# Four normalizations of the last row group spread over VectorE, GpSimd and ScalarE in a spectral-filter plus S²-MLP kernel

## The chip, the cores and the metric

The kernel runs on one core of a Trainium2 chip. The metric is the device time of one launch in microseconds (us). The core has a matrix engine (TensorE, PE in the profile, with weight loads on PEld), VectorE (DVE), ScalarE (ACT), GpSimd (POOL), and SyncE (SP), which in this kernel issues all DMAs. Every engine takes its instructions strictly in the order in which they stand in its queue; between engines, semaphores order the work.

## The reference, cut to what matters

```python
xn = layernorm(x)                                   # x: 2048 x 448, fp32
A  = irfft2(rfft2(xn) * (w_r + 1j * w_i))           # spectral filter
h  = gelu(layernorm(xn) @ w1)                       # 448 -> 448
x1 = xn + shift(h) @ w2                             # quarters of h moved by +1, -1, +2, -2 rows
B  = x1 + gelu(layernorm(x1) @ w3) @ w4             # 448 -> 1792 -> 448
return x + A + B
```

`layernorm` takes mean and variance over a row and has no learned weights.

## The kernel before

The 2048 rows are 16 blocks of 128 rows. Blocks are handled in four groups of four (`GRP`, line 22): group 0 is blocks 14, 15, 0, 1; group 1 is 2 to 5; group 2 is 6 to 9; group 3 is 10 to 13. Two blocks share one SBUF tile: blocks 10 and 11 are `xt5` (`xt_81` in the instruction rows), blocks 12 and 13 are `xt6` (`xt_82`). All matrix products run on fp16 pairs (a high part and a low part), three products for one.

Stages, in order: each group is normalized (`norm1`, line 319), turned so that features lie on partitions, and multiplied by `w1` (`w1_unit`, line 451; one unit is one block). A unit applies gelu and splits the result into high part (ACT, L461) and low part (DVE, L464), both written into `x2mem` at shifted places. When the neighbours of a block are there, a DMA transpose (L475) turns that block into a tile `h`, and `w2_tile` (line 480) multiplies it by `w2` on PE (L484, 11 matmuls of 128x448) and adds it to the block on DVE (L485, scaled by `cs`). After that come the second layer norm (`ln2`, line 488), the MLP by `w3` and `w4` (`front`, `back`), and the spectral part, whose matmuls are mixed with the MLP's. These last stages fill the time from about 70 us to the end.

`norm1(g, apply)` works out mean and variance of the four blocks on DVE (L306 to L328) and then applies them: `x * y + nm` per block, in place, on the engine that `apply` names for that block. `V` is VectorE, `P` is GpSimd (both L336, `tensor_scalar`), `A` is ScalarE (L333, an activation with scale and bias). It returns `refine` (L343 to L352), ten small GpSimd operations that sharpen the reciprocal root, which the caller runs later. `scales` (line 356) works out `cs` on GpSimd (L360 to L367).

Groups 0 to 2 are turned by PE (`T1`). Group 3 is turned by DMA: `turn(3)` (line 860) takes each block's high part on ACT (L866), its low part on DVE (L867, L868) and issues one DMA transpose per block into `xT` (L869). All DMA transposes of the kernel, L475, L520 and L869, and all plain DMAs stand in the one queue of SP.

The order in which instructions stand in each engine's queue is not written out: a scheduler places them at build time from its own estimate of the time, with priorities and with the `behind(...)` marks, which say after which instruction something may be issued. A different engine for one operation can thus move others.

PSUM banks are shared by tag, two of each: `sp` for the `w2` tiles (`pw2_0`, `pw2_1`, ...), so `pw2_2` needs the bank that L485 of `pw2_0` frees; `mm` and `acc` for the `w1` units of groups 2 and 3 (`pw1_20` is group 2, unit 0); `mm` and `tr` in turn for the first MLP tiles (`pw3_00`, `pw3_01`, ...).

Unit 0 of group 2 completes block 4 of `h` (`DONE`, line 27), which `pw2_4` reads; units 1, 2 and 3 complete blocks 5, 6 and 7. Unit 0 of group 3 completes block 8.

Of the kernel before, what the change touches and what calls it, by code (L numbers as in the profile page):

```python
# [125 lines left out]
def body(tc, nc, x, wf, w1, w2, w3, w4, c_g, c_n, c_small, out):  # L126
    V, A, P, T, SY = nc.vector, nc.scalar, nc.gpsimd, nc.tensor, nc.sync
# [40 lines left out]
    def xb(b):  # L168
        return xt[b // 2][:, b % 2]
# [130 lines left out]
    def stats(src, key, mv=None, pins=None):  # L300
        if mv is None:
            mv = pc.tile([128, 4, 2], F32, tag="mv", bufs=3, name=f"mv{key}")
        for i, s in enumerate(src):
            st = pc.tile([128, 6], F32, tag="st", bufs=4, name=f"st{key}_{i}")
            with behind(*pins[i]) if pins else contextlib.nullcontext():
                V.bn_stats(out=st, in_=s)  # L306
            V.bn_aggr(out=mv[:, i, :], in_=st)
        return mv
# [10 lines left out]
    def norm1(g, apply, pins=None):  # L319

        bs, c = GRP[g], slice(4 * g, 4 * g + 4)
        mv, a, y, nm = mva[:, c], va[:, :, c], vy[:, :, c], nma[:, c]
        stats([xb(b) for b in bs], f"a{g}", mv, pins)
        V.tensor_scalar(out=a[:, 1], in0=mv[:, :, 1], scalar1=1.0 + EPS, scalar2=EPS * EPS, op0=ALU.mult, op1=ALU.add)
        V.tensor_scalar(out=a[:, 0], in0=mv[:, :, 1], scalar1=EPS, scalar2=None, op0=ALU.add)
        V.tensor_single_scalar(vyi[:, :, c], va.bitcast(I32)[:, :, c], 1, op=ALU.logical_shift_right)
        V.tensor_scalar(out=vyi[:, :, c], in0=vyi[:, :, c], scalar1=-1, scalar2=0x5F3759DF, op0=ALU.mult, op1=ALU.add)
        i = V.scalar_tensor_tensor(out=nm, in0=mv[:, :, 0], scalar=-1.0, in1=y[:, 1], op0=ALU.mult, op1=ALU.mult)  # L328
        after["c", g] = (i.ins,)
        for k, b in enumerate(bs):  # L330
            y_, m_ = y[:, 1, k:k + 1], nm[:, k:k + 1]
            if apply[k] is A:
                i = A.activation(out=xb(b), in_=xb(b), func=AF.Identity, scale=y_, bias=m_)  # L333
                after["na", g] = (i.ins,)
            else:
                i = apply[k].tensor_scalar(out=xb(b), in0=xb(b), scalar1=y_, scalar2=m_, op0=ALU.mult, op1=ALU.add)  # L336
                after["n" if apply[k] is V else "np", g] = (i.ins,)

        q, z = (pc.tile([128, 2, 4], F32, tag=f"v{t}", bufs=2, name=f"v{t}{g}") for t in "qz")
        w, r = vw[:, :, c], vr[:, :, c]  # L340

        def refine():
            P.tensor_tensor(out=q, in0=y, in1=y, op=ALU.mult)  # L343
            P.tensor_tensor(out=q, in0=q, in1=a, op=ALU.mult)
            P.tensor_scalar(out=w, in0=q, scalar1=-10.0 / 3.0, scalar2=None, op0=ALU.add)
            P.tensor_tensor(out=w, in0=w, in1=q, op=ALU.mult)
            P.tensor_scalar(out=w, in0=w, scalar1=5.0, scalar2=None, op0=ALU.add)
            P.tensor_tensor(out=z, in0=w, in1=w, op=ALU.mult)
            P.tensor_tensor(out=z, in0=z, in1=q, op=ALU.mult)
            P.tensor_scalar(out=z, in0=z, scalar1=-0.5 * 0.375 ** 3, scalar2=1.5 * 0.375, op0=ALU.mult, op1=ALU.add)  # L350
            P.tensor_tensor(out=r, in0=z, in1=w, op=ALU.mult)
            i = P.tensor_scalar(out=gsc[:, c], in0=r[:, 1], scalar1=r1, scalar2=None, op0=ALU.mult)  # L352
            after["g", g] = (i.ins,)
        return refine
# [19 lines left out]
    @contextlib.contextmanager  # L374
    def behind(*key):
        key = key if len(key) > 1 else key[0]
        with contextlib.ExitStack() as st:
            for i in after[key]:
                st.enter_context(tc.issue_after(i))
            yield  # L380
# [501 lines left out]
    n1 = [norm1(0, [P,V,P,V])]  # L882
# [91 lines left out]
    n1[2]()  # L974
    scales(0, 3)
    with behind("a2"):
        n1 = [norm1(3, [P, P, P, P])]
    for k in range(4):
        w1_unit(2, k)
    for k in range(4):  # L980
# [166 lines left out]
```

## Time and profile before

| | |
|---|---|
| median of 3 runs | 409.3 us (408.46 to 409.64) |
| the profiled execution's own time | 408.99 us |
| its span in the profile | 407.2 us |
| granted TensorE clock over the span | 0.999 |
| busy: PE, DVE, ACT, POOL | 400.1, 335.2, 254.3, 100.0 us |
| bytes moved by DMA | 52.08 MB, mean 128 GB/s |

Busy time of PE is the time in which at least one matmul was under way by the profile, with modelled ends; matmuls are pipelined, so the time from one start to the next says how fast they go. `L12` is line 12 of the program. `pw` is a PSUM tile, `xt` the blocks, `h` the turned blocks, `xT` the turned group. Rows of SPq are instructions of SP's queue: for a DMA, the time that SP took to issue it, not the time of the transfer.

### The profile page before, as it was taken

Reading aid. Unit: us, or ns where it says so; the run is one execution under the profiler, and the core shown is the slowest. Engines: PE = TensorE matmul, PEld = TensorE weight load, DVE = VectorE, ACT = ScalarE, POOL = GpSimd, SP = SyncE. Lnnn points to the kernel's source line nnn. Section 1 sums busy time; section 2 is a strip of 40 time slices with the busy share of each in tenths; the row PEclk is TensorE's granted clock in tenths of the full one; section 3 lists DMA queues with packets and bytes.
Section 4 is the critical chain, followed back from the end, with each engine's and each line's share of the span. In section 5 each row is a group of like instructions: output and inputs, shape, how many; then the busy total and the mean of one; then the engine's idle time right before and its main releaser. Section 6 shows DMA issues by size and latency. Waiting matters only on the chain.

```text
span 407.2 us, 8731 instructions
## 1 busy us (share of the span) xinstructions
PE 400.1 (98%) x3391; PEld 297.4 (73%) x3391; DVE 335.2 (82%) x704; ACT 254.3 (62%) x431; POOL 100.0 (25%) x158
## 2 busy tenths in 40 slices
PE   8999999999999999999999999999999999999995
PEld 3555455865667777776878878787677789998994
DVE  5899799999857887988798888955999999966644
ACT  4787989864568857555798878853344455452431
POOL 6769900101137946500021111110000000000000
PEclk9999999999999999999999999999999999999999
DMA  8979965677678561636266656510012022100101
GB/s 274 382 282 187 249 128 133 131 116 158 146 194 273 205 215 30 211 110 171 72 158 163 156 144 158 130 27 2 24 68 82 12 92 90 47 2 2 45 2 46
DMA packets 54597, 52.08 MB, mean 128 GB/s; under 512 B 35678, under 2 KB 48542, under 8 KB 54556
## 3 DMA queue, kind: packets, MB, share of 16 engines
q1 hardware_dynamic: 54556, 51.53, 46.4%
q8 instruction: 26, 0.43, 0.4%
q14 instruction: 15, 0.12, 0.1%
HBM read 38.28 MB, written 3.67 MB: 103 GB/s over the span
## 4 chain that ended last, share of the span: by engine, by line
PE 87%; POOL 5%; DMA 2%; DVE 2%; ACT 2%; issue 1%; SPq 0%; POOLq 0%; ACTq 0%
PE pw L400 33%; PE acc L814 23%; PE pw L484 6%; PE side L784 4%; PE acc L784 3%; PE pu L673 3%; PE ps L573 3%; PE pe L694 2%; PE pp L628 2%; PE px L645 2%; PE py L715 2%; PE pw L420 2%; DMA w1s<-w 1%; POOL xt L336 1%; POOL w2p L938 1%
## 5 line engine op out<-in xcount | busy, mean ns | idle before, releaser
L400 PE MATMUL pw<-x2mem,w3p 128*128 128x256 f16 x1232 | 151.5, 273 | 0.0
L400 PEld LDWEIGHTS <-w3p 128*128 128x128 f16 x1232 | 118.9, 98 | 19.4
L814 PE MATMUL acc<-w4p,hf 128*128 128x448 f16 (+1 forms) x516 | 104.4, 348 | 0.0
L814 PEld LDWEIGHTS <-hf 128*128 128x128 f16 x516 | 50.1, 98 | 37.5
L732 ACT ACTIVATE pw<-pw,pe 128x512 f32<-128x512 f32 x42 | 27.4, 653 | 28.2 <-PE pw L400 28.0
L735 DVE SCALAR_TENSOR_TENSOR hf<-pw,h,hf 128x512 f16<-128x512 f32 x42 | 31.3, 745 | 12.6 <-ACT hf L734 12.4
L484 PE MATMUL pw<-w2p,h 128*128 128x448 f16 x176 | 36.1, 352 | 0.7 <-DMA h<-x2mem 0.4
L420 PE MATMUL pw<-w1p,xT 128*128 128x448 f16 x176 | 35.0, 352 | 0.0
L654 POOL TENSOR_TENSOR z<-te 128x450 f32<-128x450 f32 x16 | 15.7, 982 | 70.8 <-DVE te L652 65.9
L734 ACT ACTIVATE hf<-pw,h 128x512 f16<-128x512 f32 x42 | 28.8, 686 | 5.0 <-PE acc L814 4.0
L484 PEld LDWEIGHTS <-h 128*128 128x128 f16 x176 | 17.1, 98 | 16.6 <-DMA h<-x2mem 1.3
L750 ACT ACTIVATE hz<-g,h 128x896 f16<-128x896 f32 x14 | 14.6, 1042 | 23.0 <-DVE g L747 23.0
L784 PEld LDWEIGHTS <-hz 128*128 128x128 f16 x294 | 28.3, 98 | 0.6
L420 PEld LDWEIGHTS <-xT 128*128 128x128 f16 x176 | 17.1, 99 | 15.8 <-DVE xT L394 0.4
L635 ACT ACTIVATE pf<-pp 64x450 f16<-64x450 f32 x32 | 17.4, 543 | 12.6 <-DVE pf L636 9.6
L636 DVE TENSOR_TENSOR pf<-pp,pf 64x450 f16<-64x450 f32 x32 | 19.9, 622 | 5.1 <-ACT pf L635 4.8
L751 DVE SCALAR_TENSOR_TENSOR hz<-g,h,hz 128x896 f16<-128x896 f32 x14 | 16.1, 1147 | 6.7 <-ACT hz L750 6.7
L556 POOL TENSOR_TENSOR f<-xr 128x452 f32<-128x452 f32 x16 | 19.7, 1250 | 0.6
L564 DVE TENSOR_TENSOR xh<-f,xh 128x452 f16<-128x452 f32 x16 | 14.3, 915 | 5.5 <-ACT xh L563 5.5
L650 ACT ACTIVATE te<-px 64x450 f32<-64x450 f32 x32 | 17.3, 540 | 1.2 <-PE px L645 0.6
L744 ACT ACTIVATE g<-pw,pe 128x512 f32<-128x512 f32 x14 | 9.6, 683 | 11.4 <-PE pw L400 11.4
L553 POOL TENSOR_TENSOR xr<-xf 128x452 f32<-128x452 f32 x8 | 9.2, 1153 | 22.5 <-issue 16.6
(189 smaller groups left out, 706.0 us busy)
## 6 DMA issues: line engine op xcount, KB each, us to landing
wc<-wf SPq DMA_DIRECT2D x32, 225.0 KB, 3.7
wl<-wf SPq DMA_DIRECT2D x8, 450.0 KB, 4.3
xt<-x SPq DMA_DIRECT2D x8, 448.0 KB, 7.4
xf<-x SPq DMA_DIRECT2D x8, 448.0 KB, 4.2
loads<-x SPq DMA_DIRECT2D x7, 448.0 KB, 3.8
out<-xt SPq DMA_DIRECT2D x13, 224.0 KB, 1.9
w3raw<-w SPq DMA_DIRECT2D x3, 896.0 KB, 11.0
gn<-c_g SPq DMA_DIRECT2D x16, 128.0 KB, 3.1
```

The costliest lines, as they stand in the source:

```text
L400: T.matmul(ps_out, wp[:, wi + t, cols], xT[:, xi + t, tok], start=t == 0 and wi + xi == 0, stop=t == 3 and wi == 4)
L420: m = T.matmul(pm[:, :D], xTs[g][:, xi + t, 128 * i:128 * i + 128], w1p[:, wi + t], start=t == 0 and p == 0, stop=t == 3 and p == 2)
L484: T.matmul(pm[:, :D], h[:, k], w2p[:, w], start=n == 0, stop=n == 10)
L556: P.tensor_tensor(out=f[:, :, k:k + 2].rearrange("p b s d -> p s b d"), in0=u[:, :, 0], in1=u[:, :, 1], op=op)
L635: A.activation(out=hi, in_=src, func=AF.Copy)
L636: V.tensor_tensor(out=lo, in0=src, in1=hi, op=ALU.subtract)
L650: A.activation(out=e[64 * h:64 * h + 64], in_=px_[64 - 64 * h:128 - 64 * h, :2 * DF], func=AF.Copy)
L732: A.activation(out=pm, in_=pm, func=AF.Gelu_apprx_tanh, scale=r3)
L734: i = A.activation(out=h[:, 0], in_=pm, func=AF.Copy, scale=h3)
L735: j = V.scalar_tensor_tensor(out=h[:, 1], in0=pm, scalar=h3, in1=h[:, 0], op0=ALU.mult, op1=ALU.subtract)
L784: m = T.matmul(to, h[:, hi, 128 * blk:128 * blk + 128], b[wi], start=new and n == 0, stop=n == 2 and (last if blk in (2, 5, 3, 0) else end ...
L814: m = T.matmul(to, h[:, hi, o:o + 128], w4p[0][:, wi, f, r], start=first and f % 2 == 0 and n == 0, stop=end and f % 2 == 1 and n == 2, sk ...
```

## The change

One list of engines changes. Of the four blocks of group 3, block 10 is now normalized by VectorE, block 11 by GpSimd, block 12 by VectorE and block 13 by ScalarE; before, GpSimd took all four.

```diff
     n1[2]()
     scales(0, 3)
     with behind("a2"):
-        n1 = [norm1(3, [P, P, P, P])]
+        n1 = [norm1(3, [V, P, V, A])]
     for k in range(4):
         w1_unit(2, k)
```

The scheduler answers with another order on all engines between the normalization of group 3 and the first MLP tiles.

SP, the DMA queue, behind the last weight loads; `xT_720` is the turned group 3, `h_598` holds blocks 4 to 7, `h_916` blocks 8 to 11, `y_767` the first two blocks after `ln2`:

```order
 L223 DMA w3raw<-w 64x1792 x2
 L238 DMA w4half<-w 128x6x448
-L869 DMA_TRANSPOSE xT_720<-x_721 128x7x128 x2
-L475 DMA_TRANSPOSE h_598<-x2mem 128x7x128
-L869 DMA_TRANSPOSE xT_720<-x_721 128x7x128 x2
-L475 DMA_TRANSPOSE h_598<-x2mem 128x7x128 x3
-L475 DMA_TRANSPOSE h_916<-x2mem 128x7x128
+L869 DMA_TRANSPOSE xT_720<-x_721 128x7x128 x4
+L475 DMA_TRANSPOSE h_598<-x2mem 128x7x128 x4
 L520 DMA_TRANSPOSE x2mem<-y_767 128x7x128 x2
```

The transpose of block 4 into `h`, third in this row of transposes before, is now fifth, behind all four of group 3; that of block 8 has moved behind `y_767` and a weight load.

ACT, from the sums of squares of `w3` (L253) on; `x_721` takes the high parts of group 3, `pw_20` and `pw_21` are units 0 and 1 of group 2:

```order
 L253 ACTIVATE xr,m_169<-w3raw 128x1792 x2
+L333 ACTIVATE xt_82<-xt_82,nma,vy 128x448
+L866 ACTIVATE x_721<-xt_81 128x448
+L866 ACTIVATE x_721<-xt_82 128x448 x2
 L866 ACTIVATE x_721<-xt_81 128x448
 L460 ACTIVATE pw_20_582<-pw_20_582,gsc 128x448
-L866 ACTIVATE x_721<-xt_81 128x448
+L460 ACTIVATE pw_21_600<-pw_21_600,gsc 128x448
 L461 ACTIVATE x2mem<-pw_20_582,h_252 128x2x2x112
```

Before, the gelu of unit 0 (L460) stood behind one high part; now it stands behind the added normalization and four high parts.

DVE, at the end of the split of `w3` (L281, eight pieces); `pw_30` is unit 0 of group 3:

```order
 L485 SCALAR_TENSOR_TENSOR xt_79<-xt_79,cs,pw_7_848 128x448
-L281 SCALAR_TENSOR_TENSOR w3p<-w3raw,pe_662,w3p 128x896 x2
 L307 BN_AGGR mvb_1283<-stb_2_1290 128x2
 L281 SCALAR_TENSOR_TENSOR w3p<-w3raw,pe_662,w3p 128x896
+L464 SCALAR_TENSOR_TENSOR x2mem<-pw_30_900,h_252,x2mem 128x2x112 x2
 L306 BN_STATS stb_3_1293<-xt_79 128x6
```

The low part of unit 0 of group 3 now stands behind the last piece of `w3`; before, it stood ahead of the first. On PE, which in both programs has the same matmuls, the first MLP tiles stood as `pw3_00`, `pw3_01`, ... behind `pw2_8`; now `pw3_01` and `pw3_03` come first (43 matmuls), then 16 of `pw3_00`, and `pw2_8` after those.

## The prediction

> **What bounds the kernel now.** I read the page's busy row first, then PE's own waits, then the chain of waits and the timeline around the normalization of group 3.
>
> ```profile
> PE 400.1 (98%) x3391; PEld 297.4 (73%) x3391; DVE 335.2 (82%) x704; ACT 254.3 (62%) x431; POOL 100.0 (25%) x158
> PE wps L844 <- DVE wsrc L192: 1.2, 1, 1.2
> PE pta L389 <- POOL xt L336: 0.7, 1, 0.7
> PE pw L484 <- DMA h<-x2mem: 0.4, 2, 0.3
> PE pw L484 <- DVE xt L485: 0.3, 1, 0.3
> PE pm L260 <- DVE pt L258: 0.2, 1, 0.2
> ```
>
> PE is busy for 400.1 of 407.2 us, and the five rows are all of its waits: none behind 52 us. So behind that point each us by which PE is late is a us at the end, and nothing there can be won back. The group concerned lies just ahead of it, and two of the small waits, on L485 and on `h`, are there:
>
> ```profile
> 40.94 1.41 POOL xt L336 x2
> 42.42 0.66 POOL nm L367
> 43.08 1.76 POOL xt L336 x2
> 45.73 1.27 DVE xt L485 x2
> 47.52 3.49 DMA h<-x2mem
> 51.06 2.26 PE pw L484 x11
> ...
> 68.01 2.08 PE pw L484 x11
> 70.09 8.95 PE pw L400 x82
> 39.99 6.22 PE L420 MATMUL pw<-w1p,xT 128*128 128x448 f16 x32
> 46.46 4.32 PE L484 MATMUL pw<-w2p,h 128*128 128x448 f16 x22 [0.26 <-DVE xt L485]
> ```
>
> Eleven matmuls take 2.08 us, 0.189 each; 82 of L400 take 8.95, 0.109 each. The 32 of L420 from 39.99 could have ended issuing at 39.99 + 32 x 0.189 = 46.04, but `pw2_2` starts at 46.46: **wait A, 0.42 us**, on L485, which waits for `cs` behind GpSimd's four normalizations. `pw2_2` and `pw2_3` then issue for 4.16 us, to 50.62, and `pw2_4` starts at 51.06: **wait B, 0.44 us**, on the DMA transpose of block 4. The wait rows show a little less, since the modelled ends overlap the wait. These 0.86 us are all that the change can win.
>
> **The change part by part.** *The normalizations themselves.* GpSimd loses three, VectorE gains two, ScalarE one.
>
> ```profile
> 40.37 0.16 DVE L328 SCALAR_TENSOR_TENSOR nma<-mva,vy 128x4 f32<-128x4 f32 x1
> L336 POOL TENSOR_SCALAR xt<-xt,vy,nma x9: 703/715/1213, 8.1 to 43.8; 128x448 f32<-128x448 f32 x9
> L336 DVE TENSOR_SCALAR xt<-xt,vy,nma x5: 506/511/832, 8.0 to 28.2; 128x448 f32<-128x448 f32 x5
> L333 ACT ACTIVATE xt<-xt,nma,vy x2: 752/756/760, 18.2 to 28.6; 128x448 f32<-128x448 f32 x2
> 45.37 0.32 POOL L365 TENSOR_SCALAR cs<-cs,s 128x12 f32<-128x12 f32 x1
> 41.67 0.58 ACT L866 ACTIVATE x<-xt 128x448 f16<-128x448 f32 x1 [3.22 <-POOL xt L336]
> 44.26 0.80 DVE L464 SCALAR_TENSOR_TENSOR x2mem<-pw,h,x2mem 128x224 f16<-128x224 f32 x2
> ```
>
> GpSimd's three were 40.94 + 1.41 = 42.35 less one of 0.7, and 1.76 us behind: 2.46 us in all, so `cs` is done at 45.69 - 2.46 = 43.2 instead of 45.69. VectorE adds 2 x 0.51 = 1.02 us, from the end of the statistics (L328, 40.53) to 41.55. ScalarE adds 0.76, in an idle time of 3.22 us. L485 of `pw2_0` now stands behind three pairs of L867 and L868; with high parts on ScalarE at 41.3 + 0.5 each, the third pair ends near 43.9, L485 at 44.5. PE wants it at 46.04. Wait A goes: **-0.42 us**. If the ScalarE chain ran 1.5 us later than this, the term would be 0.
>
> *The DMA transpose of block 4.* Here lies the price. In SP's queue it was third among the transposes and is now fifth. The issues before (the rows at 44.47 and 50.49 are the second issues of the merged pairs above them):
>
> ```profile
> 38.18 0.59 SPq L238 DMA_DIRECT2D w4half<-w  x1
> 43.13 4.30 SPq L869 DMA_TRANSPOSE xT<-x  x2
> 44.47 2.96 SPq L869 DMA_TRANSPOSE xT<-x  x1
> 47.52 1.53 SPq L475 DMA_TRANSPOSE h<-x2mem  x1
> 49.15 2.58 SPq L869 DMA_TRANSPOSE xT<-x  x2
> 50.49 1.24 SPq L869 DMA_TRANSPOSE xT<-x  x1
> 51.82 7.29 SPq L475 DMA_TRANSPOSE h<-x2mem  x4
> DMA to landing us min/median/max: 2.9/3.0/5.0
> 45.00:46.00 1.00, 1.00 1.05 382
> 47.00:48.00 1.00, 1.00 0.25 27
> 49.00:50.00 1.00, 1.00 1.28 287
> ```
>
> A transpose takes SP 1.24 us to issue, but the second took 2.96. The last rows (clock, DMA share, GB/s in one us each) say why, as I read them: until 46 the engines still move `w4half`, issued at 38.18, at 382 GB/s; from 47 to 48 almost nothing moves; only then do the transposes flow. The second issue had to wait for a queue that was still full, and everything behind it in SP's queue with it. That backlog is a load that the change leaves where it is. So I keep the five issue slots as they stand: 43.13, 44.47, 47.52, 49.15, 50.49. Block 4 moves from the slot at 47.52 to the one at 50.49. Its data are ready for either: its gelu on ScalarE stands behind the added normalization and four high parts (41.3 + 4 x 0.5 = 43.3, then L460, L461), its low part on DVE is done near 47.1, against 45.06 before, and the fourth low part of group 3 near 45.8, ahead of the slot at 49.15. With the median of 3.0 from issue to landing (the row is of L475) block 4 lands at 53.5; before it landed just under 51.06. PE reaches `pw2_4` at 50.20 and waits to 53.5: wait B grows from 0.44 to 3.3. Against the start at 51.06 that is **+2.44 us**, with the gain of wait A already used up in it.
>
> Bounds. Lower: SP does not stall, four issues of 1.34 from 42.6 (the first low part is ready some 0.5 us earlier than before) let block 4 go out at 48.0, but the transposes can only flow from about 48 on. Between 49 and 50 the engines move 287 GB/s, and one transpose moves 128 x 896 x 2 bytes = 0.23 MB: 0.8 us each, five of them to 52.0, and about 0.45 us more to land: PE starts at 52.45, +1.4 us. Upper: the slots hold and the landing takes the 5.0 of the row's maximum: 55.5, +4.4. I take the slots with the median landing, since the rows on either side of that slot are ordinary ones.
>
> [...]
>
> *Work behind it.* DVE and ACT are full where the split of `w3` runs:
>
> ```profile
> 60.00:65.00 5.00, 5.00 (x28) 2.55 (x27) 5.00 (x9) 5.00 (x8) 0.00 (x0) 1.00 0.88 143
> 65.00:70.00 5.00, 5.00 (x28) 2.61 (x27) 5.00 (x6) 5.00 (x9) 0.00 (x0) 1.00 0.39 145
> 70.18 1.13 DVE L281 SCALAR_TENSOR_TENSOR w3p<-w3raw,pe,w3p 128x896 f16<-128x896 f32 x1
> ```
>
> (PE, PEld, DVE, ACT, POOL busy in 5 us each.) The 1.02 us added to DVE lie in this stretch's queue, but PE comes 2.44 us later. The tightest place: the low part of `pw1_30` (two of 0.44 us) has moved behind the eighth L281, which ended at 71.31. With 1.02 and up to 1 us for other operations that moved ahead of it, it is done at 72.3 to 73.3. `pw3_00` needs its bank behind `pw3_01` and `pw3_03`: the last L420 issued to 68.01, now 70.45, plus 43 x 0.109 = 75.1. In time. The transpose of block 8 goes out behind the same low part, at 73.4 at the latest, and lands 3.0 later, at 76.4; `pw2_8` comes at 75.1 + 16 x 0.109 = 76.9. In time by 0.5. Term 0, up to +1.0 if the DVE chain is 1.5 us later than this. If PE were not late, this cover would be gone, and the same chain would cost up to 2 us here.
>
> **Sum**: +2.44 + 0 = +2.4 us, 407.2 + 2.4 = 409.6 of span. The profiled execution took 408.99, 1.8 more than its span, and lies 0.3 under the median of 409.3; put on the median: **411.7 us**.
>
> **The rivals.** *Block 4 is not late.* If SP's stall belongs to the second transpose alone and the engines flow earlier, the fifth issue can go when block 4 is ready, 47.6, and land at 50.6, 0.4 earlier than before: 408.9 us. If waits A and B both went, 408.4. For it: the last L869s need no data that come late. Against it: the 27 GB/s from 47 to 48, during which two transposes were already issued and did not move. It is the end on the other side: it decides from the point at which block 4 lands before 51.0.
>
> *The full engines set a second wait.* The order by which `pw3_00` and `pw2_8` hang on the split of `w3` costs another 1 to 2 us: 412.7 to 413.7. For it: two engines at 5.00 of 5 us; against it: PE's own lateness.
>
> *The clock falls in the wait.* A PE pause of 3.3 us is longer than any of PE's wait rows above (1.2 at most), and at the kernel's start PE is slow:
>
> ```profile
> 1.20:6.70 5.50, 5.48 (x13) 1.96 (x14) 1.00 0.88 291
> 6.70:9.50 2.80, 2.80 (x14) 1.18 (x12) 1.00 1.04 344
> ```
>
> The first 13 warming matmuls (L844, x13 in the first column) take 0.42 us each, the next 14 only 0.20. If the wait put PE back there, some 5.5 us at half speed would cost 2.7 more: 414.4. [...]
>
> **How the numbers follow.** Forecast 0.65; not late 0.15; second wait 0.12; clock 0.08. The forecast's own range, +1.4 to +3.4, is 410.7 to 412.7. The range of 8 in 10 reaches into the rivals: 409.4 to 413.8, which leaves out most of the first and the clock case. Under 0.3% (1.2 us) no change can be told from none. Faster by that much would need more than both waits: 0.03. The case that is not late, and a tail of the forecast under +1.2, give within 0.3%: 0.17. Slower: 0.80.
>
> **What would show it.** Right: no wait on L485 near 46; four L869 in a row on SP, one of them near 3 us; the transpose of block 4 issued near 50.5 and landing past 53; one PE wait of 3 us on `h`; no PE wait behind it; L844's speed nowhere again; a shift of 2.4 us that stays constant from `pw2_4` to the end. Wrong: block 4 issued by 48; PE waits for L464, `w3p` or block 8 past 70 us; matmuls of 448 columns at 0.38 us behind the wait.

## The result, and the profile after

The changed kernel took 412.37 us (median of 5 runs, 411.33 to 413.72) against 409.3: a ratio of 1.0085, 95% interval 1.0069 to 1.0101. It is slower by 3.1 us; 411.7 was forecast. The profiled execution is the fastest of the five, 411.33 us with a span of 409.6, 2.4 over the span before.

PE's own waits after the change (engine, tile, line, releaser: us in total, times, longest):

```profile
PE pw L484 <- DMA h<-x2mem: 3.8, 1, 3.8
PE wps L844 <- DVE wsrc L192: 1.2, 1, 1.2
PE pm L260 <- DVE pt L258: 0.9, 1, 0.9
PE pta L389 <- POOL xt L336: 0.7, 1, 0.7
```

The wait on L485 is gone, the one on `h` has grown from 0.4 to 3.8, and nothing behind it waits. The timeline around it, PE and SP's queue (start, duration, line, count of merged instructions, in brackets the idle time ahead):

```profile
46.37 4.33 PE L484 MATMUL pw<-w2p,h 128*128 128x448 f16 x22
54.50 2.25 PE L484 MATMUL pw<-w2p,h 128*128 128x448 f16 x11 [3.80 <-DMA h<-x2mem]
38.76 0.59 SPq L238 DMA_DIRECT2D w4half<-w  x1
43.22 5.12 SPq L869 DMA_TRANSPOSE xT<-x  x2
43.22 8.08 SPq L869 DMA_TRANSPOSE xT<-x  x4
51.39 1.25 SPq L475 DMA_TRANSPOSE h<-x2mem  x1
```

`pw2_2` and `pw2_3` now run without a break, then PE stands still until 54.50. On SP, the first two transposes of group 3 take 5.12 us to issue (1.23 for the first, 3.78 for the second, with a short gap), and all four take 8.08. Block 4's follows at 51.39, the fifth, and lands at 54.46. Here each stage of the path is 0.6 to 1.0 us later than forecast: the `w4half` load was issued at 38.76 instead of 38.18, and landed 10.8 us later instead of 10.5. The traffic shows the backlog again (us, clock, share, GB/s):

```profile
46.00:47.00 1.00, 1.00 1.05 382
...
48.00:49.00 1.00, 1.00 0.50 30
...
50.00:51.00 1.00, 1.00 1.28 287
```

So the path is the forecast one. But the five runs do not look like one wait with noise: the profiled one has a mean TensorE clock of 1.0, three have 0.995 to 0.996 and took 412.3 to 412.5, one has 0.991 and took 413.72. Of the 52 runs of the kernel before whose clock is on record beside the experiments, 51 lie at 0.998 to 1.0, and one at 0.994 (410.55 us).

### The profile page after: what moved, and what is told of

Its sections match the earlier page's. It is cut to its first block, busy times and chain, and to the rows that moved or that the text cites. A ratio compares the mean times of both kernels' runs of the same rounds, so it can differ in the third digit from the quotient of the medians.

```text
span 409.6 us, 8730 instructions
## 1 busy us (share of the span) xinstructions
PE 399.4 (98%) x3391; PEld 297.3 (73%) x3391; DVE 337.4 (82%) x706; ACT 255.2 (62%) x432; POOL 99.6 (24%) x155
## 3 DMA queue, kind: packets, MB, share of 16 engines
q1 hardware_dynamic: 54556, 51.53, 46.3%
## 4 chain that ended last, share of the span: by engine, by line
PE 86%; POOL 5%; DVE 3%; DMA 2%; ACT 1%; issue 1%; SPq 1%; POOLq 0%
PE pw L400 33%; PE acc L814 23%; PE pw L484 6%; PE side L784 4%; PE acc L784 3%; PE pu L673 3%; PE ps L573 3%; PE pe L694 2%; PE pp L628 2%; PE px L645 2%; PE py L715 2%; PE pw L420 2%; DMA xt<-x 1%; POOL w2p L938 1%; POOL xt L336 1%
## 5 line engine op out<-in xcount | busy, mean ns | idle before, releaser
L420 PE MATMUL pw<-w1p,xT 128*128 128x448 f16 x176 | 35.2, 352 | 0.1
L420 PEld LDWEIGHTS <-xT 128*128 128x128 f16 x176 | 17.1, 99 | 16.1 <-DVE xT L394 0.5
```

What stands on the lines that cost most here:

```text
L420: m = T.matmul(pm[:, :D], xTs[g][:, xi + t, 128 * i:128 * i + 128], w1p[:, wi + t], start=t == 0 and p == 0, stop=t == 3 and p == 2)
```

## The experiments

Times of the kernel before are from the same chip in the same set of runs: 408.36 us for the first four kernels, 408.45 for the next four, 408.36 for the last two.

**The changed kernel again**, beside the first experiments.

> The changed kernel once more, for its spread and its clock. Theory (one PE wait on the DMA transpose of block 4, which SP's order makes late): one PE wait of 3.3 to 4.0 us on h near 50 to 54, none over 0.3 us behind it, about 3 us over the kernel before. Rival (the clock falls in that wait): runs over 412 us show a granted clock under 0.998, and matmuls of 448 columns take 0.38 us from one start to the next for some us right behind the wait; without it the spread of the five runs has another source.

412.16 us (410.11 to 413.97, 6 runs), ratio 1.0088 (1.0059 to 1.0118). Two runs at a clock of 1.0: 410.11 and 410.5. Two at 0.995 to 0.996: 412.13 and 412.2. Two at 0.991: 413.62 and 413.97. The profiled run is one at full clock; block 4 goes out at 50.52, and PE idles for 3.35 us. The two parts of the loss separate here: some 2 us that each run pays, and more in runs whose clock fell.

**Block 4's transpose put back to third place.** The normalization stays spread, and PE, VectorE, ScalarE and GpSimd have the changed kernel's orders row for row; only the rows of SP's queue differ.

```diff
-            d = SY.dma_start_transpose(out=xTs[g][:, :, 128 * i:128 * i + 128], in_=h)
+            with behind("h", 2, 0) if i > 1 else contextlib.nullcontext():
+                d = SY.dma_start_transpose(out=xTs[g][:, :, 128 * i:128 * i + 128], in_=h)
```

> The changed kernel with its four engines, but the last two DMA transposes of group 3 stand behind that of block 4 in SP's queue, which is third again as before the change. Theory: block 4 goes out near 47.5 and lands near 51, the PE wait on h is under 1 us, and all of the loss goes: 408.5 to 409.6 us, no more than the kernel before. Rival (VectorE's and ScalarE's added work costs the time): still 411.5 to 412.5 us.

407.93 us (407.79 to 408.34, 11 runs), ratio 0.9988 (0.9979 to 0.9998), every clock 0.999 or 1.0. SP's queue and PE's wait in its trace:

```profile
42.98 4.70 SPq L870 DMA_TRANSPOSE xT<-x  x2
47.78 2.81 SPq L475 DMA_TRANSPOSE h<-x2mem  x2
50.64 2.63 SPq L870 DMA_TRANSPOSE xT<-x  x2
46.24 4.33 PE L484 MATMUL pw<-w2p,h 128*128 128x448 f16 x22
51.28 0.93 PE L484 MATMUL pw<-w2p,h 128*128 128x448 f16 x4 [0.71 <-DMA h<-x2mem]
```

The whole loss sits in the order of SP's queue. The 4.70 us of the first row hold no stall: the second transpose is now block 11's, whose low part ends on VectorE at 46.40; it goes out at 46.46 and takes 1.22 us.

The median is 0.4 us under that of the kernel before, with an interval just clear of 1. That is the size of wait A, but the trace doesn't show it as such. Counted from the start of the 32 matmuls of L420 (40.19 here, 39.99 before), `pw2_2` starts after 6.05 us instead of 6.47, so wait A is won; but PE then waits 0.71 us for block 4 instead of 0.28, and `pw2_4` starts after 11.09 us against 11.07. Where the 0.4 us come from is open.

**The normalization of before, with the changed kernel's order on SP.**

```diff
+    turn(3)
     for k in range(4):
         w1_unit(2, k)
...
-    turn(3)
...
+            with behind("t", 3) if (g, i) == (2, 0) else contextlib.nullcontext():
+                d = SY.dma_start_transpose(out=hT[b // 4][:, :, 128 * (b % 4):128 * (b % 4) + 128],
```

> The kernel before, GpSimd still normalizing all four blocks, but block 4's DMA transpose stands behind all four of group 3 as in the changed kernel. The scheduler then puts the 11 matmuls of unit 0 of group 3 ahead of pw2_4 on PE, which fill 2.08 us of the wait. Theory: PE waits near 50.6 for the fourth transpose of group 3, which lands near 52, so some 1.0 us over the kernel before, 410.0 to 410.6. Rival (engines): nothing is added to an engine, so 409.3 as before.

408.69 us (408.39 to 409.28, 11 runs), ratio 1.0007 (0.9998 to 1.0016): less than expected. Block 4 was issued as late as forecast, but the scheduler, to which the added mark made it look late too, had put the 11 matmuls of `pw1_30` ahead of `pw2_4`:

```profile
50.97 1.29 SPq L476 DMA_TRANSPOSE h<-x2mem  x1
51.72 0.38 PE L260 MATMUL pm<-pt,ones 128*128 128x1 f32 x2 [0.78 <-DVE pt L258]
51.97 2.24 PE L420 MATMUL pw<-w1p,xT 128*128 128x448 f16 x11
54.05 2.26 PE L485 MATMUL pw<-w2p,h 128*128 128x448 f16 x11
```

Issued at 50.97, it landed at 54.01, and PE came to it at 54.05 from other work. With other matmuls ahead of `pw2_4` in PE's queue, the late block 4 cost only 0.3 us. As a test of the SP order alone this run is spoilt by PE's changed order.

**The `w4half` load issued behind block 4**, so that it no longer stands ahead of the transposes in SP's queue.

```diff
-        load_w4(8, 6)
...
+    with behind("h", 2, 0):
+        load_w4(8, 6)
```

> The changed kernel with all four transposes of group 3 ahead of block 4, but the 1344 KB load of w4half is issued behind block 4's transpose instead of ahead of group 3's. Theory (SP's second issue waits for a queue still full of that load): no transpose takes SP more than 1.5 us, block 4 goes out by 48.5 and lands by 51.5, 408.5 to 409.5 us. If the place in the queue alone cost the time, block 4 would still go out near 50.5: 411 to 412 us. Rival (engines): 412 us. A wait of ScalarE for the later load may cost up to 1 us in any case.

410.2 us (409.47 to 410.68, 7 runs), ratio 1.004 (1.0025 to 1.0054), every clock 0.999 or 1.0.

```profile
42.74 5.64 SPq L869 DMA_TRANSPOSE xT<-x  x4
48.48 2.59 SPq L475 DMA_TRANSPOSE h<-x2mem  x2
51.12 0.58 SPq L238 DMA_DIRECT2D w4half<-w  x1
PE pw L484 <- DVE x2mem L464: 1.3, 1, 1.3
PE pw L484 <- DMA h<-x2mem: 0.5, 1, 0.5
```

The four transposes now issue in 5.64 us instead of 8.08, none of them stalled, and land sooner; the stall has moved with the load, to the second transpose behind it (4.11 us, from 53.30). The table of DMA issues, whose last column is the median from issue to landing, has for the changed kernel

```profile
xT<-x SPq DMA_TRANSPOSE x4, 5.0
```

and for this one

```profile
xT<-x SPq DMA_TRANSPOSE x4, 2.6
```

The backlog of the load is what held SP. The wait for block 4 falls to 1.3 us (the row names L464, but that was done long before; block 4 landed at 51.49, where PE starts). The total missed the expected range by 0.7 us: the row on `h` is a second wait, at 75 us on block 8, and PE's starts show a further 0.3 at 79. The late load makes them. ScalarE waits for it before its part of the split of `w3`:

```profile
58.20 0.95 ACT L253 ACTIVATE xr<-w4half 128x896 f16<-128x896 f32 x1 [2.09 <-DMA w4half<-w]
```

That part starts at 59.67, against 57.97 in the run with block 4 third, and block 8's transpose goes out at 72.27 against 70.64. That run has no wait of PE behind 52 us, although PE is just as little late in it (`pw2_4` at 51.28, here at 51.53). From 61 us on the orders of PE and VectorE changed a little too.

**Three of group 3's transposes ahead of block 4's**, between the two kernels, by another split of the normalization (against the kernel before).

```diff
-        n1 = [norm1(3, [P, P, P, P])]
+        n1 = [norm1(3, [V, P, V, P])]
```

> The kernel before with another split of group 3's normalization, VectorE and GpSimd in turn (VectorE, GpSimd, VectorE, GpSimd), so that SP's order has three of group 3's transposes ahead of block 4's: between the kernel before (two) and the change (four). Theory (each transpose ahead costs block 4 one slot of 1.2 to 1.5 us, and the clock falls only behind a wait of about 3.5 us): PE waits 1.6 to 2.8 us for block 4, every run has a clock of at least 0.998, and the median is 0.5 to 1.5 us over the kernel before. Rival (the loss is all or nothing: it comes whole as soon as the second transpose of group 3 meets the full queue): the wait is 3.3 to 4.0 us, with runs at a lower clock, and the median 3 to 3.8 us over. Rival (what costs is the work given to ScalarE, which this split leaves out): no loss beyond 0.3 us.

409.12 us (408.8 to 409.51, 11 runs), ratio 1.0016 (1.0006 to 1.0026), every clock 1.0.

```profile
42.95 6.20 SPq L869 DMA_TRANSPOSE xT<-x  x3
49.24 1.25 SPq L475 DMA_TRANSPOSE h<-x2mem  x1
52.31 2.25 PE L484 MATMUL pw<-w2p,h 128*128 128x448 f16 x11 [1.87 <-DMA h<-x2mem]
```

PE's order is the changed kernel's. With one transpose less ahead, block 4 is issued one slot earlier, at 49.24, PE waits 1.87 us, and the loss is 0.7 us. The cost goes by slots, not all or nothing, and with a wait of this length all eleven runs kept the full clock.

**Dummy matmuls in the wait.** SP's queue keeps its order up to 73 us. Behind the wait the scheduler set PE's and VectorE's orders anew (`pw2_5` now follows `pw2_4` at once), so not all else is equal, as the expectation took for granted.

```diff
+        for i in range(14 if b == 4 else 0):
+            T.matmul(pm[:, :D], wsrc[:, 0:128], wsrc[:, :D], start=True, stop=True)
         for n, (k, w) in enumerate([(k, w) for k in range(3) for w in (k, k + 7)] + [(3, 10)] + [(k, k) for k in (3, 4, 5, 6)]):
```

> The changed kernel with 14 dummy matmuls of 448 columns (on a tile of zeros, into pw2_4's own bank, which the first real matmul overwrites) queued on PE between pw2_3 and pw2_4. They add work only inside the wait: 14 by 0.19 us is 2.6 us, and block 4 lands when it did. Theory (the loss has two parts: a wait of 3.5 to 4.0 us that costs 2 to 2.4 us net, and a fall of TensorE's clock behind it in most runs, which costs 2 to 3.5 us more in those): PE stands idle for at most 1.5 us at a time, every run has a clock of at least 0.998, the spread of the runs shrinks from 3.9 us to about 1, and the median is that of the changed kernel's runs at full clock, 1.7 to 2.5 us over the kernel before, instead of 3 to 3.8. Rival (the runs at a clock of 0.991 to 0.996 have another cause than this wait): about two runs of three still show such a clock, and the median stays 3 to 3.8 us over the kernel before.

410.42 us (409.87 to 410.61, 6 runs), ratio 1.004 (1.0024 to 1.0056), every clock 0.999 or 1.0.

```profile
46.12 4.33 PE L486 MATMUL pw<-w2p,h 128*128 128x448 f16 x22
50.28 2.62 PE L484 MATMUL pw<-wsrc 128*128 128x448 f16 x13
53.86 4.33 PE L486 MATMUL pw<-w2p,h 128*128 128x448 f16 x22 [0.63 <-DMA h<-x2mem]
```

`pw2_4` still starts only when block 4 lands, and no wait has come behind it, so the cost of the wait stays: +1.97. But PE idles 0.63 us at a time instead of 3.3, no run is left at a lower clock, and the spread shrinks from 3.9 us to 0.74. Useless work made the median 1.1 to 1.7 us lower than the changed kernel's in two other sets (411.54 and 412.16). The second part of the loss hangs on PE's idleness there.

**A longer wait, first try**: two of the blocks of the `w4half` load loaded twice.

```diff
+        load_w4(8, 2)
         load_w4(8, 6)
```

> The changed kernel with two of the six blocks of the w4half load (0.46 MB, about 1.6 us at 288 GB/s) loaded twice, ahead of the load itself, so that SP's queue is longer by them when the transposes of group 3 and block 4 are issued; all orders are the changed kernel's. Theory (the transposes wait for the queue to empty, PE waits for block 4, and the clock falls behind a wait of more than about 3.5 us): the wait on h grows from 3.5 to 4.0 us to 5 to 7, no run is left at a clock of 0.998 or more, and the median is 5 to 9 us over the kernel before. Rival on the queue (the slot in SP's order alone decides, not what the queue holds): the wait stays at 3.3 to 4.0 us, and the median 3 to 3.8 us over. Rival on the clock (its falls have nothing to do with this wait): about a third of the runs stays at a clock of 1.0 however long the wait is.

413.27 us (411.11 to 414.97, 6 runs), ratio 1.0109 (1.008 to 1.0139); two runs at a clock of 1.0, four at 0.991 to 0.996. The expectation was wrong in two points. The two loads write the same place, so SP waited for the first to land (the second was issued at 46.48); and PE's order was not the changed kernel's, `pw1_30` stood ahead of `pw2_4`. The one long wait became two:

```profile
54.09 3.13 PE L420 MATMUL pw<-w1p,xT 128*128 128x448 f16 x11 [3.25 <-DMA xT<-x]
58.47 4.04 PE L484 MATMUL pw<-w2p,h 128*128 128x448 f16 x11 [1.25 <-DMA h<-x2mem]
54.00:55.00 1.00, 1.00 1.28 285
55.00:56.00 1.00, 0.66 0.85 193
56.00:57.00 1.00, 0.50 0.58 119
...
61.00:62.00 1.00, 0.50 0.89 166
62.00:63.00 1.00, 0.93 1.05 204
```

As a dose it tells nothing, but its profile caught the fall (the first number behind the comma is the granted clock). PE resumes at 54.09 after 3.25 us; the clock is halved from about 55.3 (0.66 of that us) to 62.1. `pw2_4`'s 11 matmuls take 4.04 us, not 2.25.

**A longer wait, second try**: the added load goes into a tile of its own.

```diff
+    again = pc.tile([128, 2, D], F32, name="again")
...
+        SY.dma_start(again, w4v[:, 8:10])
         load_w4(8, 6)
```

> The changed kernel with an added load of 0.46 MB (two blocks of w4, into a tile of its own that nothing reads) ahead of the w4half load in SP's queue; unlike the run with the repeated blocks, it overlaps no other load, so SP waits for no landing, and PE's order is the changed kernel's: one wait, on block 4. Theory (the transposes wait until the queue has emptied, PE waits for block 4, and the clock falls behind a wait of 3.3 us or more, the more surely the longer it is): the wait on h grows by about 1.6 us to 5.0 to 5.7, no run of the kernel is left at a clock of 0.998 or more, the clock rows show half speed behind the wait, and the median is 5 to 7.5 us over the kernel before. Rival on the queue (the slots alone decide): the wait stays at 3.3 to 4.0 us, the median 2 to 4 over. Rival on the clock (its falls have nothing to do with the length of the wait): a third of the runs stays at a clock of 1.0 and these runs are 3.6 us over the kernel before.

414.37 us (413.83 to 414.71, 4 runs), ratio 1.0148 (1.0127 to 1.0169). All four runs have a lower clock: 0.996, 0.992, 0.991, 0.991.

```profile
42.84 9.29 SPq L870 DMA_TRANSPOSE xT<-x  x4
55.27 3.90 PE L485 MATMUL pw<-w2p,h 128*128 128x448 f16 x11 [4.79 <-DMA h<-x2mem]
55.00:56.00 1.00, 0.62 1.02 192
56.00:57.00 1.00, 0.50 0.90 174
57.00:58.00 1.00, 0.50 0.82 159
58.00:59.00 1.00, 0.68 0.66 127
59.00:60.00 1.00, 1.00 0.00 0
```

A longer backlog, with all orders as they were, makes SP's four issues longer (9.29 us) and the wait on block 4 1.0 to 1.5 us longer (4.79, a little under the 5.0 expected), and the clock fell in all four runs. In the profiled one it was at half for 0.76 + 1 + 1 + 0.64 = 3.4 us, from the moment at which PE resumed.

**The changed kernel a third time**, beside the last.

> The changed kernel as it stands, beside it on the same chip, to count once more how many of its runs have the lower clock and, if the profiled one is among them, to see where the clock falls. Theory (wait of 3.3 to 4.0 us, then in about two runs of three a stretch at half clock): the runs lie in two groups, at a clock of 1.0 and 1.7 to 2.5 us over the kernel before, and at 0.991 to 0.996 and 3.5 to 5.5 us over; the share of the second group is under that of the run with the longer wait. Rival (a steady loss with noise): one group.

411.54 us (410.41 to 413.33, 6 runs), ratio 1.0081 (1.0055 to 1.0107): three runs at 1.0 (410.41 to 410.84), one at 0.996 (412.24), two at 0.991 (413.2 and 413.33). The profiled run was one at full clock again; in its timeline

```profile
50.49 1.25 SPq L475 DMA_TRANSPOSE h<-x2mem  x1
53.58 2.25 PE L484 MATMUL pw<-w2p,h 128*128 128x448 f16 x11 [3.30 <-DVE x2mem L464]
```

block 4 goes out at 50.49 and PE idles for 3.30 us, ended by the landing at 53.53 (again not by the L464 that the row names).

**Block 4 third and the load behind it**, both remedies together.

> The changed kernel with block 4's transpose third again (as in the run that put it there) and also the w4half load behind block 4 (as in the run that moved the load). Theory: with neither the queue full nor four transposes ahead, block 4 is issued before 47 us and its wait on PE is gone, which is worth another 0.7 to 0.9 us over the run with block 4 third; the later load costs 0.9 us again at blocks 8 and 9. Sum: 0.5 us under to 0.4 over the kernel before. Rival (the late w4half load costs nothing here, since the waits at 75 and 79 us came from the four transposes): 0.8 to 1.4 us under the kernel before.

410.59 us (410.23 to 411.45, 6 runs), ratio 1.005 (1.0035 to 1.0065): worse than block 4 third alone, no better than the later load alone, and missed by all that was expected of it. Rows of SP's queue and of PE's waits:

```profile
50.07 0.58 SPq L238 DMA_DIRECT2D w4half<-w  x1
52.08 4.61 SPq L475 DMA_TRANSPOSE h<-x2mem  x1
PE pw L484 <- DMA h<-x2mem: 0.7, 2, 0.5
PE acc L814 <- ACT hf L734: 0.7, 1, 0.7
PE acc L814 <- DVE hf L735: 0.4, 1, 0.4
```

Block 4 goes out at 47.43, not before 47, since block 11's transpose stands ahead of it and block 11's low part ends at 46.04. The wait for block 4 is nearly gone (0.24 us of idling at 50.3), but the load's backlog has only moved: now the issue of a transpose behind it takes 4.61 us. ScalarE waits 1.85 us for the load, and the waits for blocks 8 and 9 come again, at 75 and 79 us; the load makes them, since this run differs by its later place alone from the one with block 4 third, and that one has none. Two more waits come at 114, in the MLP. How the later load reaches as far as those was not followed.

## Why the prediction was right, and where it was not

**The place and the mechanism** were right. Wait A went. Block 4's transpose went out fifth, behind a second transpose of group 3 that took 3.4 to 3.8 us to issue. With the order put back, the loss was gone; with the backlog taken away, SP's stall was gone. In the third set block 4 was issued at 50.49 and landed at 53.53, both within 0.05 us of the forecast, and the idle time was the 3.3 forecast; in the first profile, with a later `w4half` load, it was 3.8. The stall on SP follows the backlog: gone without it, longer with more of it (four issues in 5.64, 8.08 and 9.29 us). The time from issue to landing of these four goes the same way, a median of 5.0 us behind the load and 2.6 without it. No run shows what the issuing engine itself waits for; that it is room in the queue is a reading.

**The net term**, +2.44 us, was sized well for a run at full clock. The six such runs among the changed kernel's 17 lie 1.75 to 2.48 us over their medians of before, 2.1 on average, and the run with dummy matmuls lies at +1.97.

**The work behind it** at 0 was right: no wait of PE behind `pw2_4` in any of the three profiles of the changed kernel. That PE's lateness is its cover, without which the same chain would cost up to 2 us, was not borne out: with block 4 third, `pw2_4` is 0.2 us late, all orders but SP's are the changed kernel's, and PE waits for nothing behind 52 us. Block 8's transpose then goes out at 70.64 instead of 73.54. *Block 4 is not late* and *the full engines set a second wait* both fell.

**What failed is the clock.** The prediction gave its fall a chance of 0.08 and expected "L844's speed nowhere again". That chance was the author's estimate: the kernel before has no wait of PE over 1.2 us, so its profile could not show what a wait of 3.3 us does. The fall came in 11 of the 17 runs. Over the kernels tried, the longest idle time of PE there and the runs with a clock under 0.998 were:

| kernel | idle, us | runs with the lower clock |
|---|---|---|
| block 4 third, load behind it | 0.24 | 0 of 6 |
| the kernel before | 0.28 | 1 of 52 |
| dummy matmuls in the wait | 0.63 | 0 of 6 |
| block 4 third | 0.71 | 0 of 11 |
| SP's new order, old normalization | 0.78 | 0 of 11 |
| `w4half` load later | 1.3 | 0 of 7 |
| block 4 fourth | 1.87 | 0 of 11 |
| repeated blocks (two waits) | 3.25 | 4 of 6 |
| the change | 3.3 to 3.8 | 11 of 17 |
| one long wait | 4.79 | 4 of 4 |

The idle times are those of the profiled runs; those of the changed kernel's runs at a lower clock are not known, and the one run of the kernel before has no explanation here. One and the same program, the changed kernel, kept its clock in 6 runs and lost it in 11.

**What the traces show of the fall.** Two of the profiles caught it, both of a kernel other than the changed one. Their moments are worked out from the clock in rows of 1 us:

| profile | PE's idle time there, us | PE resumes at | clock |
|---|---|---|---|
| block 4 fourth | 1.87 | 52.31 | stays |
| the change, third set | 3.30 | 53.58 | stays |
| the change again | 3.35 | 53.62 | stays |
| the change, first | 3.80 | 54.50 | stays |
| repeated blocks | 3.25, then 1.25 | 54.09, then 58.47 | half from 55.32 to 62.14 |
| one long wait | 4.79 | 55.27 | half from 55.24 to 58.64 |

With the repeated blocks the clock fell 1.2 us after PE had resumed, with the one long wait just as PE resumed. A wait of 3.25 us was followed by a fall in one profile, and waits of 3.30 to 3.80 us were not in three others, so the length of the wait alone doesn't decide. After PE's last matmul the clock falls too: 3.2 us behind it in the profile before (402.83 to 406.01), 4.6 us in the first profile after (406.28 to 410.91). What decides whether a wait of this length is followed by a fall was not shown.

**The size of the fall** was put at 2.7 us, from the 5.5 us of slow matmuls at the start. That stretch ends with the first rise (6.65 us in the profile before; ahead of it the trace has no clock record, so the 1.00 in the prediction's row says nothing) and differs from run to run (4.73 us in the first profile after); it is no measure of a fall. The two stretches seen lasted 3.40 and 6.82 us, and the mean clocks of these two runs are 0.996 and 0.992, close to the two groups of the changed kernel's runs. By the times, the six runs at 0.995 to 0.996 lie 3.5 us over before on average, 1.4 more than those at full clock, and the five at 0.991 lie 5.0 over, 2.9 more. In the run with the longer stretch, PE idled for another 1.25 us within it. Whether a rest of the wait does the same in the changed kernel stays open: no profile of it caught a fall.

**What was luck.** The median of 412.37 is a mixture of the forecast and of the rival *the clock falls in the wait*, in the same kernel. The forecast time of 411.7 lies between the two groups of runs. The forecast's own range, 410.7 to 412.7, holds the run at full clock (411.33) and also three of the four others, because the runs at 0.995 to 0.996 lie only some 1.4 us over those at full clock: that a median with the fall in it lies there is no merit of the terms. The span of 409.6 in the first profile is the forecast one by luck, too. PE's last 36 matmuls, before and after:

```profile
398.10 4.73 PE L814 MATMUL acc<-w4p,hf 128*128 128x448 f16 x36
401.55 4.73 PE L814 MATMUL acc<-w4p,hf 128*128 128x448 f16 x36
```

They start 3.4 us later, as `pw2_4` does (54.50 against 51.06): the shift is constant to the end of PE's work, as forecast, but 1.0 us more than the 2.44. The span grew by 2.4 only, since the profiled run before went on for 9.1 us from these matmuls' start and the eleven other profiles for 8.0 to 8.2. Why it did was not followed. In the two other profiles of the changed kernel the shift is 2.5 to 2.6 us, at `pw2_4` and at the last matmuls alike.

## What to carry to other kernels

When work becomes ready earlier on one engine, look at what it can overtake in a DMA queue that is shared, and what that queue still holds: a transfer that PE needs next can fall behind several that it doesn't need yet, each of them a slot (1.24 us here), and a slot behind a backlog lasts longer (3.78 us here). If an engine with a strict order will wait for it, put other work ahead of the wait, or hold the others back with a mark; here one mark took the whole loss of 3 us away. Price a long wait of PE as two terms, the wait itself and a stretch at half clock that may follow it (here in none of 11 runs with a wait of 1.87 us, in 11 of 17 with one of 3.3 to 3.8); if the times of one kernel lie in groups, look at the granted clock of each run before seeking a cause elsewhere.

## What the hardware showed that was not expected

- With one wait of 3.3 to 3.8 us in the middle of a busy kernel, 11 of 17 runs had a mean TensorE clock of 0.991 to 0.996. The two traces that show such a fall, behind waits of 3.25 and 4.79 us, have the clock at half for 6.82 and 3.40 us.
- With 14 matmuls on zeros in that wait the clock stayed up in all six runs, and the matmuls cost no time that shows (+1.97 us, against +2.1 for the changed kernel's runs at full clock).
- SP's issue of a DMA transpose, 1.24 us otherwise, took 2.96 us before, 3.78 after and 4.61 in the run with both remedies, each time 2 to 6.3 us behind the issue of the 1344 KB `w4half` load, and all that stood behind it on SP waited as well. Issued 8.1 us behind that load, with block 4 third, one took 1.22.
